# A first load split over two queues, a last batch left in one part and a new table of ranks in a relu² attention kernel with adapters

## The chip, the cores and the metric

The kernel runs on one core of a Trainium2 chip. TensorE (PE in the rows) does the matmuls and writes PSUM. VectorE (DVE) and ScalarE (ACT) read PSUM and do all elementwise work. GpSimd (POOL) and SyncE (SP) issue transfers, POOL those that cast on the way. The metric is the device time of one execution in microseconds, as the median of several runs.

## What is computed

Eight batches of twelve heads, 448 tokens of 64 values, go through an attention with a squared relu in place of a softmax. The result, 3584 tokens of 768 values, goes through eight adapters of rank 16, of which each token takes its two best.

```python
scores = q @ k.transpose(0, 1, 3, 2) / sqrt(64)
attn   = np.maximum(scores, 0.0) ** 2 / 448
x      = (attn @ v).transpose(0, 2, 1, 3).reshape(3584, 768)
logits = x @ w_gate                       # 8 experts
w      = softmax of the two largest logits
out    = x + sum over the two of  w * ((x @ A[e]) @ B[e])
```

## The kernel before

The program is a list of small operations (`build`). Each has the engines that may do it, a duration that the planner assumes, what it depends on, buffers that it takes and gives back, and a rank. `schedule` (L78) walks through time with these assumed durations and hands each free engine the ready operation with the lowest rank. What comes out is a fixed order of instructions for each engine. Each engine then runs its own row strictly in that order. Transfers have their place in the rows of SP, ACT or POOL.

A batch has three "quads" of four heads; a tile of q, k or v is one quad (128 partitions, 2 x 448 values). For each quad:

- **Load** (L250): POOL issues two casting transfers, one for each half of the partitions, float32 in memory to bf16 on chip. The very first q and k are done otherwise (`first`, L263): two float32 transfers each, q from SP and k from ACT, and then a cast, q on VectorE, k on ScalarE (L274).
- **Transposes** (L353): 28 small matmuls for q, 28 for k, into one pair of PSUM banks, copied out by VectorE in one piece (L362). The first quad is copied out in two pieces, q by VectorE and k by ScalarE (L368).
- **QK** (L394): seven steps `j`, each four matmuls of 64 x 448 into a pair of banks. **Relu** (L414 on ScalarE, L416 on VectorE) takes such a pair, 128 x 896, to bf16. **Square** (L432, VectorE) does two steps at once, 128 x 1792.
- **PV** (L449): seven steps accumulate in another pair of banks, which is copied to `xt`, one bank at a time (L473).

For each token tile of 128 (28 tiles, `gate` and `outputs`): the gate matmuls (L490), a chain of small operations on VectorE with a sigmoid on ScalarE between them (L511 to L534), a transpose of the weighted low-rank values (L555) copied out as `zT` (L568), then the output stage: 24 small matmuls that put `x` into a pair of banks (L587), the float32 matmuls with B on top (L602), two copies to `osb` (L621), and the stores from SP (L632). One tile at a time may hold the banks of the output stage (`cap`, "o": 1).

The eight banks are shared by all of this; QK may hold up to three pairs. In the last batch the 448 query columns are cut into 320 and 128 (`PARTS`): all three quads run first for the 320 and then for the 128, so that token tiles 24 to 26 can be finished while the 128 are still being worked on.

Of the kernel before, what the change touches and what calls it, by code (L numbers as in the profile page):

```python
# [9 lines left out]
F32 = mybir.dt.float32  # L10
BF16 = mybir.dt.bfloat16
# [15 lines left out]
PARTS[NB - 1] = ((0, 320), (320, S))  # L27

C = dict(
    slack=0.24419, switch=0, third=5.2529, dve_relu=0.32574, relu_until=400, qk=-3.132, sq=6, pv=5.6586,  # L30
    xt=6.5598, tp=-15.842, tpe=5.1552, gate_mm=0, gate=-6.1261, zt=11.533, zte=14, id=0.77356, out=3.6939,
    pace=6.4673,
)
POOLS = dict(qT=5, a1=4, a2=9, zp=2, zT=3, osb=6, w=3, q=4, k=4, v=6)

MODE_SWITCH = 0.27
HOP = 0.05
LAT = {"PE": 0.165, "ACT": 0.19, "DVE": 0.084, "POOL": 0.0, "SP": 0.0}
# [28 lines left out]
class Dma:  # L67


    def __init__(self, rate=0.33, fixed=2.0):  # L70
        self.rate, self.fixed, self.free = rate, fixed, 0.0

    def land(self, t, mb):
        self.free = max(self.free, t + 0.9) + mb / self.rate
        return self.free + self.fixed - 0.9


def schedule(ops, c=C):  # L78
# [5 lines left out]
    level = dict(POOLS)  # L84
    freed = {b: 0.0 for b in range(8)}
    used = {"s": 0, "t": 0, "p": 0, "m": 0, "y": 0, "o": 0}
    cap = {"s": 3, "t": 1, "p": 2, "m": 2, "y": 1, "o": 1}
# [17 lines left out]
    def choose(o):  # L105
# [3 lines left out]
        slots = sorted((x for x in range(0, 8, 2) if x in freed and x + 1 in freed),  # L109
# [11 lines left out]
        busy = 4 - len(slots) - used["s"]  # L121
        if not slots or busy >= 2:
            return None
# [25 lines left out]
    while left:  # L149
# [9 lines left out]
        for e in free:  # L159
# [6 lines left out]
            if e == "PE":  # L166
                if mode is not None and o.mode != mode:
                    st += MODE_SWITCH
                mode = o.mode
# [25 lines left out]
            for u in o.users:  # L195
                u.missing -= 1
                u.ready = max(u.ready, st if u.after is o else back)
# [19 lines left out]
def build(k=None, c=C):  # L217
# [32 lines left out]
    def load(b, w, q, deps):  # L250
# [8 lines left out]
        o = op(("POOL",), 1.3, fn, deps=deps, kind="load", take=(nm,))  # L259
# [3 lines left out]
    def first(w):  # L263

        nm = "qkv"[w]
        eng = ("SP", "ACT")[w]

        def dma():
            for g in range(2):
                (nc.sync, nc.scalar)[w].dma_start(out=k.raw[w][g * PH : g * PH + PH],  # L270
                                                  in_=k.qkv[w][0, g, :, 0:2, :])

        def cast(cp):
            cp(new(nm, (nm, 0, 0), [128, 2, S], BF16), k.raw[w])  # L274

        d = op((eng,), 0.8, dma, kind="load", rank=-50.0)
        d.mb = 4 * S * 64 * 4e-6
        if w == 0:
# [516 lines left out]
```

## Time and profile before

| | us |
|---|---|
| median of 3 runs (202.75 to 203.67) | 203.2 |
| time of the profiled execution | 201.0 |
| its span, first to last instruction | 199.2 |
| first relu starts | 13.92 |
| last QK matmul ends | 181.53 |
| last relu ends | 181.96 |
| last output copy ends | 194.50 |

Shares of busy time over the whole span: TensorE 81%, VectorE 84%, ScalarE 83%. The granted TensorE clock is 0.999 of full speed on average. Idle time of an engine in these rows has a releaser: the instruction or transfer that ended the wait.

### The profile page before, as it was taken

The page shows a single profiled execution, that of the slowest core. Times are in us where ns is not written, and L with a number is a line of the kernel's source. Part 1 is how long each engine was busy: PE and PEld are TensorE (multiplying, and loading weights), DVE is VectorE, ACT ScalarE, POOL GpSimd, SP SyncE. Part 2 cuts the span into 40 slices and gives each one's busy share as a digit, 9 for nine tenths or more (in the row PEclk, how much of TensorE's full clock was granted, in tenths as well). Part 3 has the DMA queues.
Part 4 walks back from the last instruction along what each step waited for, and adds up shares of the span by engine and source line. Part 5 has one row for each costly group of instructions (what it writes and reads, how often), then busy time and mean ns, then how long its engine had stood idle before and what let it go on. Part 6 is the DMA issues. An engine that isn't in the chain of part 4 may idle for free.

```text
span 199.2 us, 10411 instructions
## 1 busy us (share of the span) xinstructions
PE 162.1 (81%) x4664; PEld 109.0 (55%) x4664; DVE 166.6 (84%) x278; ACT 164.5 (83%) x254; POOL 87.9 (44%) x150
## 2 busy tenths in 40 slices
PE   0056887685999799979987999799999999999990
PEld 0043665363667366646654666466655576585650
DVE  0039999898999999799989999999899799896830
ACT  0167957999999899989999999989999999795330
POOL 8339978989856265726364445642200000000000
PEclk9999999999999999999999999999999999999999
DMA  5997999999999988998899959996540450543655
GB/s 129 225 207 88 141 170 181 160 194 172 178 160 219 206 113 133 225 201 110 144 191 198 126 110 198 213 146 134 129 89 3 121 125 3 143 103 81 164 132 189
DMA packets 26733, 29.66 MB, mean 149 GB/s; under 512 B 4416, under 2 KB 22848, under 8 KB 26688
## 3 DMA queue, kind: packets, MB, share of 16 engines
q0 software_dynamic: 21344, 16.27, 59.1%
q1 hardware_dynamic: 5056, 12.26, 22.0%
q8 instruction: 36, 0.59, 1.3%
q10 hardware_dynamic: 288, 0.46, 0.9%
q14 instruction: 9, 0.07, 0.1%
HBM read 34.23 MB, written 11.01 MB: 227 GB/s over the span
## 4 chain that ended last, share of the span: by engine, by line
PE 46%; ACT 18%; DVE 18%; issue 8%; DMA 6%; SPq 1%; DVEq 0%; ACTq 0%
ACT a L414 15%; PE ps L602 14%; PE ps L449 12%; PE ps L394 9%; DVE a L432 8%; DMA raw<-in_q_dram 4%; PE ps L353 3%; PE ps L555 3%; PE ps L587 3%; DVE a L416 2%; DMA out_dram<-osb 2%; ACT osb L621 2%; DVE qT L362 2%; PE ps L490 1%; DVE zT L568 1%
## 5 line engine op out<-in xcount | busy, mean ns | idle before, releaser
L414 ACT ACTIVATE a<-ps 128x896 bf16<-128x896 f32 (+2 forms) x178 | 139.7, 879 | 9.8 <-PE ps L394 7.3
L432 DVE TENSOR_TENSOR a<-a 128x1792 bf16<-128x1792 bf16 (+3 forms) x96 | 90.5, 967 | 3.5 <-ACT a L414 3.1
L394 PE MATMUL ps<-qT 64*64 64x448 bf16 (+2 forms) x756 | 68.5, 350 | 13.7 <-ACT a L414 9.4
L394 PEld LDWEIGHTS <-qT 64*64 64x64 bf16 x756 | 30.6, 108 | 36.0 <-issue 25.9
L449 PE MATMUL ps<-a,v 64*64 64x448 bf16 (+2 forms) x756 | 43.8, 329 | 2.7 <-issue 0.9
L602 PE MATMUL ps<-B,zT 64*64 64x384 f32 x448 | 45.8, 489 | 0.0
L256 POOL DMA_DIRECT2D v<-in_v_dram x48 | 28.9, 611 | 34.8 <-PE ps L394 15.3
L256 POOL DMA_DIRECT2D q<-in_q_dram x46 | 27.9, 618 | 13.6 <-PE ps L394 6.3
L449 PEld LDWEIGHTS <-v 64*64 64x64 bf16 x756 | 25.0, 106 | 12.2 <-issue 6.9
L256 POOL DMA_DIRECT2D k<-in_k_dram x46 | 28.1, 627 | 7.2 <-DMA q<-in_q_dram 4.9
L362 DVE COPY qT<-ps 128x1792 bf16<-128x1792 bf16 x23 | 24.9, 1085 | 2.0 <-PE ps L353 1.4
L621 ACT COPY osb<-ps 128x384 f32<-128x384 f32 x38 | 18.7, 549 | 6.8 <-PE ps L602 5.9
L353 PE MATMUL ps<-identb,q 64*64 64x64 bf16 x672 | 12.3, 199 | 12.5 <-DVE q L274 10.4
L473 DVE CAST xt<-ps 128x448 bf16<-128x448 f32 (+2 forms) x38 | 20.7, 568 | 0.8 <-PE ps L449 0.7
L353 PEld LDWEIGHTS <-q 64*64 64x64 bf16 x672 | 11.6, 114 | 17.7 <-DVE q L274 10.4
L602 PEld LDWEIGHTS ps<-B,zT 64*64 64x64 f32 x448 | 16.5, 134 | 4.4 <-issue 3.0
L621 DVE COPY osb<-ps 128x384 f32<-128x384 f32 x18 | 10.0, 555 | 5.8 <-PE ps L602 4.6
L587 PEld LDWEIGHTS <-xt 64*64 64x64 bf16 x672 | 11.0, 108 | 5.3 <-issue 3.5
L416 DVE TENSOR_SCALAR a<-ps 128x896 bf16<-128x896 f32 (+1 forms) x11 | 11.3, 1028 | 2.9 <-PE ps L394 2.9
L490 PE MATMUL ps<-awg,xt 128*128 128x136 bf16 x168 | 13.0, 224 | 0.4 <-DVE osb L621 0.4
L587 PE MATMUL ps<-identb,xt 64*64 64x64 bf16 x672 | 11.7, 194 | 1.0 <-ACT osb L621 0.9
L490 PEld LDWEIGHTS <-xt 128*128 128x128 bf16 x168 | 10.0, 98 | 4.4 <-issue 4.1
(35 smaller groups left out, 96.8 us busy)
## 6 DMA issues: line engine op xcount, KB each, us to landing
out_dram<-osb SPq DMA_DIRECT2D x56, 192.0 KB, 3.7
v<-in_v_dram POOLq DMA_DIRECT2D x48, 112.0 KB, 4.6
q<-in_q_dram POOLq DMA_DIRECT2D x46, 112.0 KB, 4.9
k<-in_k_dram POOLq DMA_DIRECT2D x46, 112.0 KB, 5.2
B<-in_moe_B_dram SPq DMA_DIRECT2D x2, 384.0 KB, 10.1
raw<-in_k_dram ACTq DMA_DIRECT2D x2, 224.0 KB, 5.5
raw<-in_q_dram SPq DMA_DIRECT2D x2, 224.0 KB, 6.3
a_raw<-in_moe_A_dram POOLq DMA_DIRECT2D x1, 192.0 KB, 3.8
```

Source lines behind the costliest of these rows:

```text
L256: nc.gpsimd.dma_start(out=t[g * PH : g * PH + PH], in_=k.qkv[w][b, g, :, 2 * q : 2 * q + 2, :])
L353: nc.tensor.transpose(k.ps_b[sl * PH : sl * PH + PH, m.banks[g], (w * J + j) * PH : (w * J + j) * PH + PH], T["qk"[w], b, q][r, sl, j * PH ...
L362: nc.vector.tensor_copy(t.rearrange("p g w x -> p g (w x)"), k.ps_b[:, m.banks[0] : m.banks[0] + 2, : 2 * S])
L394: nc.tensor.matmul(out=bank(o, sl)[g * PH : g * PH + PH, at : at + w], lhsT=t[r, g, 1, j * PH : j * PH + PH], rhs=t[r, g, 0, x0:x1], start ...
L414: nc.scalar.activation(out, flat(qk_ops[n], w), ACTF.Relu, scale=k.relu_scale)
L432: nc.vector.tensor_mul(a2, T["a1", g0], T["a1", g0])
L449: nc.tensor.matmul(out=bank(head, g)[sl * PH : sl * PH + PH, :w], lhsT=vn[r, sl, j * PH : j * PH + PH], rhs=T["a2", g0][r, i, sl * w : sl ...
L473: evac(w, lambda cp, g=g: cp(k.xt[:, g * QUADS + q, b * S + x0 : b * S + x1], bank(src, g)[:, :w]), deps=[pv_ops[n]], free=[(src, g)], ran ...
L490: nc.tensor.matmul(out=bank(zops[0])[:, t * ZW : t * ZW + ZW], lhsT=k.xt[:, do, 128 * tiles[t] : 128 * tiles[t] + 128], rhs=k.awg[:, do, : ...
L587: nc.tensor.matmul(out=bank(o_id, r)[tok * PH : tok * PH + PH, do * PH : do * PH + PH], lhsT=k.xt[rr, do, c0 + tok * PH : c0 + tok * PH + PH],
L602: nc.tensor.matmul(out=bank(o_id, r)[tok * PH : tok * PH + PH, : DO * PH].rearrange("p (o d) -> p o d", o=DO), lhsT=T["zT", g0][rr, zi, h, ...
L621: cp(T["osb", tl].rearrange("p (o r d) -> p r o d", r=2, d=PH)[:, r], bank(o_id, r)[:, : DO * PH].rearrange("p (o d) -> p o d", o=DO))
```

## The change

- **First q and k.** q alone comes uncast, its two halves from two queues (SP and ACT, one transfer each), and VectorE casts it. The first k becomes an ordinary casting load on POOL, ahead of the others. The transposes of the first k are cut into 3 and 4 steps, and VectorE copies them out in two pieces, after q's.
- **Sigmoid's table.** A sigmoid of eight values stands at the head of ScalarE's row (`warm`), so that the table it needs is loaded there; the later load goes.
- **Last batch.** `PARTS` no longer cuts it.
- **xt copies.** Up to step 147 the two banks of a PV result are copied by one instruction.
- **Output stage.** Two tiles may hold banks there (`ocap=2`).
- **B.** In the planner its load depends on that of A.
- **Buffers and ranks.** `a1` 4 to 5, `a2` 9 to 12, all ranks new, assumed durations and the assumed speed of transfers changed, a successor on the same engine may follow at once.

```diff
-PARTS[NB - 1] = ((0, 320), (320, S))
 C = dict(
-    slack=0.24419, switch=0, third=5.2529, dve_relu=0.32574, relu_until=400, qk=-3.132, sq=6, pv=5.6586,
...
+    a12=(5, 12), merge_x=147, merge_o=0, ocap=2, sqs=(2,), slack=0.032648, switch=3.8275, third=6,
+    dve_relu=0.39442, relu_until=400, qk=-5.753, sq=6.7076, pv=4.9427, xt=7.7968, tp=-16.052,
...
-POOLS = dict(qT=5, a1=4, a2=9, zp=2, zT=3, osb=6, w=3, q=4, k=4, v=6)
+POOLS = dict(qT=5, a1=C["a12"][0], a2=C["a12"][1], zp=2, zT=3, osb=6, w=3, q=4, k=4, v=6)
...
-    cap = {"s": 3, "t": 1, "p": 2, "m": 2, "y": 1, "o": 1}
+    cap = {"s": 3, "t": 1, "p": 2, "m": 2, "y": 1, "o": c.get("ocap", 1)}
...
+    def first():
+        def dma(eng, g):
+            eng.dma_start(out=k.raw[g * PH : g * PH + PH], in_=k.qkv[0][0, g, :, 0:2, :])
+        def warm():
+            nc.vector.memset(k.warm, 0.0)
+            nc.scalar.activation(k.warm, k.warm, ACTF.Sigmoid)
+        ds = [op(("SP",), 0.8, lambda: dma(nc.sync, 0), kind="load", rank=-50.0),
+              op(("ACT",), 0.8, lambda: dma(nc.scalar, 1), kind="load", rank=-50.0)]
+        op(ACT, 1.4, warm, rank=-49.0)
...
+        if (b, q) == (0, 0):
+            cut, evs = 3, []
+            m1 = op(PE, 0.1, lambda: mm(1, 0, cut), deps=[loaded[b, 1, q], m], after=m, mode="64", kind="tp",
...
+            for i, (d, x0, x1) in enumerate(((m, 0, S), (m1, S, S + cut * PH), (m2, S + cut * PH, 2 * S))):
+                evs.append(op(DVE, dve(2 * (x1 - x0), 1.92), lambda x0=x0, x1=x1: piece(x0, x1),
...
+        if n < c["merge_x"]:
+            return [
+                evac(2 * w, lambda cp: cp(k.xt[:, q::QUADS, b * S + x0 : b * S + x1], pair(src)[:, :, :w]),
+                     deps=[pv_ops[n]], free=[(src, 0), (src, 1)], rank=pv_ops[n].rank + c["xt"])
+            ]
...
-    b_load = op(("SP",), 0.8, b_fn, kind="load")
...
+            b_load = op(("SP",), 1.4, b_fn, deps=[a_load], kind="load")
```

The start of ScalarE's row before (a name's number is its buffer; `waits` names the engine or transfer queue whose semaphore it waits for):

```order
L270 DMA raw_104<-in_k_dram 64x2x448 x2
L274 ACT_TABLE_LOAD [waits DMAHW2_49]
L274 CAST k_0_162<-raw_104 128x896 [waits DMAHW0_49]
L368 COPY qT_0_160<-ps 128x2x448 [waits DVE_49,PE_49]
L414 ACTIVATE a_0_211<-ps 128x896 [waits PE_49]
```

The same place now:

```order
L273 DMA raw<-in_q_dram 64x2x448
L277 ACT_TABLE_LOAD
L277 ACTIVATE warm<-warm 1x8 [waits DVE_49]
L429 ACTIVATE a_0_205<-ps 128x896 [waits PE_49]
L429 ACTIVATE a_2_239<-ps 128x896 [waits PE_49] x2
```

k's cast and its copy have left ScalarE, and the table load stands ahead of all data and waits for none. On SP one transfer of q is left; B's two follow it directly in both rows, without a wait.

POOL's loads at the start, before:

```order
L256 DMA q_1_118<-in_q_dram 64x2x448 x2
L256 DMA k_1_121<-in_k_dram 64x2x448 x2
L256 DMA v_0_124<-in_v_dram 64x2x448 x2
L256 DMA q_2_157<-in_q_dram 64x2x448 x2
L256 DMA k_2_164<-in_k_dram 64x2x448 [waits DMASW0_49]
L256 DMA k_2_164<-in_k_dram 64x2x448 [waits DMASW1_49]
```

And now:

```order
L262 DMA k_0_116<-in_k_dram 64x2x448 x2
L262 DMA q_1_119<-in_q_dram 64x2x448 x2
L262 DMA k_1_122<-in_k_dram 64x2x448 x2
L262 DMA v_0_155<-in_v_dram 64x2x448 x2
L262 DMA q_2_189<-in_q_dram 64x2x448 [waits DMASW0_49]
L262 DMA q_2_189<-in_q_dram 64x2x448 [waits DMASW1_49]
```

The first k stands in the place that q of the second quad had; every later load has moved back by one place. The ninth transfer waits for the first to land, in both.

The end of ScalarE's row before, from its last relus (`sg` is the sigmoid of a gate, `zT` and `osb` the copies around the output stage):

```order
L414 ACTIVATE a_188_5110<-ps 128x256
L621 COPY osb_5120<-ps 128x6x64
L527 ACTIVATE sg_5180<-t_5174 128x16
L527 ACTIVATE sg_5186<-t_5182 128x8
L621 COPY osb_5198<-ps 128x6x64
L473 CAST xt<-ps 128x128 x2
L527 ACTIVATE sg_5323<-t_5321 128x8
L621 COPY osb_5341<-ps 128x6x64
L568 COPY zT_5344<-ps 128x2x2x64
L621 COPY osb_5388<-ps 128x6x64
L621 COPY osb_5427<-ps 128x6x64
L621 COPY osb_5464<-ps 128x6x64
```

And now:

```order
L429 ACTIVATE a_166_4807<-ps 128x896 x2
L648 COPY osb_4846<-ps 128x6x64
L648 COPY osb_4885<-ps 128x6x64
L493 CAST xt<-ps 128x448
L648 COPY osb_4924<-ps 128x6x64
L547 ACTIVATE sg_4988<-t_4978 128x16
L547 ACTIVATE sg_4996<-t_4992 128x8
L648 COPY osb_5016<-ps 128x6x64
L648 COPY osb_5101<-ps 128x6x64
L648 COPY osb_5168<-ps 128x6x64
L648 COPY osb_5205<-ps 128x6x64
L648 COPY osb_5214<-ps 128x6x64
```

Six output copies stood behind the last relu, now eight do, and the gates of the last four tiles come behind the last full-width `xt` copy.

## Rows read from the trace of the kernel before

**Rows 1.** Stretches: length, busy us (count) of each engine, granted clock, transfer share, GB/s

```profile
13.90:182.00 168.10, 148.44 (x4259) 100.00 (x4255) 157.59 (x247) 156.88 (x238) 80.56 (x133) 1.00 0.85 144
24.00:35.00 11.00, 8.94 (x288) 6.62 (x285) 11.00 (x14) 7.47 (x10) 9.05 (x17) 1.00 1.19 174
```

**Rows 2.** Timeline of the start: start, length, engine, instruction [idle before, releaser]

```profile
9.17 1.28 ACT L274 ACT_TABLE_LOAD   x1 [9.17 <-DMA raw<-in_k_dram]
9.69 0.63 DVE L274 CAST q<-raw 128x896 bf16<-128x896 f32 x1 [8.12 <-DMA raw<-in_q_dram]
...
11.02 0.62 DVE L368 COPY qT<-ps 128x896 bf16<-128x896 bf16 x1 [0.70 <-PE ps L353]
...
11.69 0.59 PE L353 MATMUL ps<-identb,k 64*64 64x64 bf16 x28 [0.73 <-DVE qT L368]
12.33 0.91 ACT L368 COPY qT<-ps 128x896 bf16<-128x896 bf16 x1 [0.92 <-PE ps L353]
...
13.28 1.33 PE L394 MATMUL ps<-qT 64*64 64x448 bf16 x12 [1.00 <-ACT qT L368]
```

**Rows 3.** Transfers issued at 0.74: size, us from issue to landing

```profile
raw<-in_k_dram ACTq DMA_DIRECT2D x1, 224.0 KB, 3.5
raw<-in_q_dram SPq DMA_DIRECT2D x1, 224.0 KB, 4.5
```

**Rows 4.** The same view: issued from 1.4 to 2.8, POOL's first three and SP's second, third

```profile
q<-in_q_dram POOLq DMA_DIRECT2D x1, 112.0 KB, 6.4
...
raw<-in_q_dram SPq DMA_DIRECT2D x1, 224.0 KB, 8.0
...
B<-in_moe_B_dram SPq DMA_DIRECT2D x1, 384.0 KB, 9.4
q<-in_q_dram POOLq DMA_DIRECT2D x1, 112.0 KB, 8.1
k<-in_k_dram POOLq DMA_DIRECT2D x1, 112.0 KB, 9.8
```

**Rows 5.** Groups by shape: count, busy us, mean ns of one, idle before and releasers

```profile
L414 ACT ACTIVATE a<-ps 128x896 bf16<-128x896 f32 x137 | 118.8, 977 | 7.9 <-PE ps L394 6.4 <-issue 1.3
L432 DVE TENSOR_TENSOR a<-a 128x1792 bf16<-128x1792 bf16 x73 | 77.4, 1083 | 2.1 <-ACT a L414 1.9
...
L414 ACT ACTIVATE a<-ps 128x640 bf16<-128x640 f32 x21 | 14.0, 710 | 0.9 <-ACT a L414 0.4 <-PE ps L394 0.3
...
L432 DVE TENSOR_TENSOR a<-a 128x1280 bf16<-128x1280 bf16 x10 | 7.8, 818 | 0.4 <-ACT a L414 0.4
...
L414 ACT ACTIVATE a<-ps 128x256 bf16<-128x256 f32 x20 | 7.0, 388 | 1.0 <-PE ps L394 0.7 <-ACT a L414 0.2
...
L432 DVE TENSOR_TENSOR a<-a 128x512 bf16<-128x512 bf16 x10 | 4.1, 423 | 1.0 <-ACT a L414 0.9
```

**Rows 6.** Timeline of ScalarE around the second table load

```profile
34.22 13.20 ACT L414 ACTIVATE a<-ps 128x896 bf16<-128x896 f32 x16 [1.27 <-issue]
47.44 1.28 ACT L527 ACT_TABLE_LOAD   x1
48.73 0.22 ACT L527 ACTIVATE sg<-t 128x24 f32<-128x24 f32 x1
```

**Rows 7.** Who waited for whom: us in total, times, longest

```profile
PE ps L394 <- ACT a L414: 9.4, 23, 0.9
```

**Rows 8.** Timeline of the end

```profile
181.28 0.25 PE L394 MATMUL ps<-qT 64*64 64x128 bf16 x4
...
185.09 0.95 PE L449 MATMUL ps<-a,v 64*64 64x128 bf16 x56
...
186.91 0.38 PE L587 MATMUL ps<-identb,xt 64*64 64x64 bf16 x24
...
187.34 1.52 PE L602 MATMUL ps<-B,zT 64*64 64x384 f32 x16
...
193.94 0.56 DVE L621 COPY osb<-ps 128x384 f32<-128x384 f32 x1 [1.00 <-PE ps L602]
```

More of the change, by code (lines that the diff above doesn't have):

```diff
@@ L108, in choose @@
             return None
-        slots = sorted((x for x in range(0, 8, 2) if x in freed and x + 1 in freed),
+        slots = sorted((x for x in range(0, c.get("nb", 8), 2) if x in freed and x + 1 in freed),
                        key=lambda x: max(freed[x], freed[x + 1]))
@@ L196, in schedule @@
                 u.missing -= 1
-                u.ready = max(u.ready, st if u.after is o else back)
+                u.ready = max(u.ready, st if u.after is o or u.engs == (e,) and o.kind != "load" else back)
                 if not u.missing:
@@ L257, in fn @@
                                     in_=k.qkv[w][b, g, :, 2 * q : 2 * q + 2, :])
-        o = op(("POOL",), 1.3, fn, deps=deps, kind="load", take=(nm,))
+        o = op(("POOL",), 1.17, fn, deps=deps, kind="load", take=(nm, "lane"), give=("lane",))
         o.mb = 4 * S * 64 * 4e-6
         return o
[L263 to L278, printed above, removed]
-            return evac(2 * S, cast, engs=DVE, rate=1.92, deps=[d], take=(nm,), rank=-50.0)
-        return evac(2 * S, cast, engs=ACT, deps=[d], take=(nm,), rank=-50.0)
+    def first():
[7 more added lines that the diff above has]
+        op(ACT, 1.4, warm, rank=-49.0)
+        for d in ds:
+            d.mb = 2 * S * 64 * 4e-6
+        return evac(2 * S, lambda cp: cp(new("q", ("q", 0, 0), [128, 2, S], BF16), k.raw), engs=DVE, rate=1.92,
+                    deps=ds, take=("q",), rank=-50.0)
     def sel_fn():
@@ L346, in tp, with mm @@
         rank = first_use[b, q] + c["tp"]
-        def mm(w):
-            for j in range(J):
+        def mm(w, j0=0, j1=J):
+            for j in range(j0, j1):
                 for g in range(2):
@@ L615, in outputs, with ev_all @@
         evs = []
-        for r in range(2):
+        def ev_all(cp):
+            cp(new("osb", ("osb", tl), [128, 128 * DO], F32).rearrange("p (o r d) -> p r o d", r=2, d=PH),
+               pair(o_id)[:, :, : DO * PH].rearrange("p r (o d) -> p r o d", d=PH))
+        if tl < c["merge_o"]:
+            evs.append(evac(2 * DO * PH, ev_all, deps=[prev], free=[(o_id, 0), (o_id, 1)], rank=v + c["out"]))
+        for r in range(2) if not evs else ():
             def ev(cp, r=r):
@@ L683, in build @@
     zuse = {g[0]: len(g) for g in groups}
-    xdeps, seen = {}, set()
+    xdeps, seen, nx = {}, set(), {}
     def finish(n):
@@ L693, in finish @@
             xt_ops.setdefault(col, []).extend(x)
+        nx.update({o: 1 / len(x) for o in x})
         for tl in range(NT):
             both = [xt_ops.get(128 * tl + h * 64, []) for h in range(2)]
-            if tl not in xdeps and all(len(x) == 2 * QUADS for x in both):
+            if tl not in xdeps and all(sum(nx[o] for o in x) == QUADS for x in both):
                 xdeps[tl] = list(dict.fromkeys(both[0] + both[1]))
@@ L751 @@
     h.g_raw = const.tile([128, DO, E], BF16)
-    h.raw = [const.tile([128, 2, S], F32, name=f"raw{w}") for w in range(2)]
+    h.raw = const.tile([128, 2, S], F32)
+    h.warm = const.tile([1, 8], F32)
     ctx.enter_context(tc.manual_schedule())
```

69 lines of the change are left out of this document (37 added, 32 removed).

## The prediction

> **What bounds the kernel now.** I read the stretches first. From the first relu (13.9) to the last (182.0) VectorE is busy for 157.6 and ScalarE for 156.9 of 168.1 us, TensorE for 148.4 [rows 1]. So over 84% of the span the two elementwise engines set the pace together, each with about 11 us of idle time. Much of ScalarE's idle time lies in one place: from 24 to 35 it works 7.5 of 11 us while VectorE works all 11 [rows 1]. The waits agree: QK waits 23 times for ScalarE to give back a bank pair, 9.4 us in total [rows 7]. Ahead of that stretch stand 13.9 us in which no relu can run, and behind it 17 us that end the program; there one chain decides. So I take three terms: start, middle, end.
>
> The start, read from the timeline: q's cast waits until 9.69 for q's second half, then come transposes, VectorE's copy to 11.64, k's transposes (they wait for that copy), ScalarE's copy to 13.24, and QK at 13.28 [rows 2]. The table load at 9.17 stands beside this chain: k's cast behind it is done before VectorE's copy lets the k transposes go. The end: after the last QK matmul (181.53) TensorE works nearly without a gap, a tile every 1.75 us, to 193.93; then copies to 194.50 and stores to 199.2 [rows 8].
>
> **Start: -2.6 us.** Both first halves that were issued at 0.74, one from each queue, landed 3.5 and 4.5 us later [rows 3]; q's second half, behind the first on SP, took 8.0 from 1.56 [rows 4]. Now q's halves are the first ones of their two queues. So q lands at 0.74 + 4.5 = 5.25 instead of 9.6. Cast 0.63, transposes 0.59, copy 0.62 [rows 2] and three handovers of 0.05, as between 11.64 and 11.69, end at 7.25. Then k decides, since it comes through POOL. POOL's first load took 6.4 us for one half and 8.1 for the other [rows 4], issued at 1.43 and about 2.1: landed at 7.8 and 10.2. That is the late bound for k, which takes this place. For the early bound, q's own path (7.25) lets the k transposes start at once. B is not moved: the planner's new dependence gives no wait in SP's row, B follows q directly and is in flight with k (before, its first half landed 9.4 us after its issue [rows 4]). But k's float32 halves, 448 KB that shared the engines with POOL's first load, are gone from the other queues. I take 9.0, nearer to the late bound because B stays. From there: transposes 0.59, the two pieces copied by VectorE 0.62 in all, three handovers, 1.4 together: QK at 10.4 instead of 13.28, a gain of 2.9. The bounds are 10.2 + 1.4 = 11.6, a gain of 1.7, and 7.25 + 1.4 = 8.65, a gain of 4.6. The split of the k copies earns nothing: VectorE's second piece has no wait of its own in the order and the first QK waits once, so both come after all 28 transposes; its price is one of the handovers above.
>
> What is queued behind: TensorE's row has the second quad's q transposes after three QK steps. That q stands where the second quad's k stood, which landed at about 2.73 + 9.8 = 12.5 for its first half [rows 4]; without k's float32 bytes ahead of it, earlier. Should it land at 12.5 to 13.5, TensorE stands still for 1 to 2 us, with three relus of 0.98 to cover. That takes back 0 to 1.2; I take 0.3, since the relus ahead of it hide most. So the start gives 2.6, and its low end is 1.7 - 1.2 = 0.5.
>
> **Middle: -3.7 us.** Three things leave it. (a) The cut last batch. A relu of 640 and one of 256 hold ScalarE for 14.0/21 + 7.0/20 = 1.02 us, one of 896 for 118.8/137 = 0.87 [rows 5]: 0.15 for each of 21 steps, 3.2 us. Squares: 7.8/10 + 4.1/10 = 1.19 against 77.4/73 = 1.06 [rows 5], ten times 0.13: 1.3 us. (b) The sigmoid's table load, 1.28 us in the middle of a full ScalarE [rows 6]; in its new place, behind the issue of one transfer, some eight idle microseconds of ScalarE hide it until the first relu at about 11. (c) The xt copies: 54 become 27; one instruction less is worth at most the same 0.15, 4.0 us. Together 9.8 us of work on two engines that share it, 4.9 each. That is the upper end, because it takes every instruction as if it stood alone. In a full row they overlap: 16 relus take 13.20 us, (13.20 - 0.98)/15 = 0.815 apart [rows 6], of which 896 x (0.977 - 0.388)/640 per element = 0.82 is already the whole; so the fixed cost of one instruction in a full row may be near nothing. The order also moves three relus and four output copies from ScalarE's row to VectorE's, which gives up as much in xt copies; that shifts work between two engines that are equally full, and I cost it at nothing. Lower end: (b) and half of (a), 3.5 us, 1.8 each. I take 3.7, in the upper half, because the groups of the last batch do have waits between their short pieces, 0.9 to 1.0 us each for three of the four [rows 5], and because fewer relus are given to VectorE early, where it alone is full [rows 1].
>
> More `a1` and `a2` buffers and new ranks change who waits, not the work, and I cost them at nothing. They could win back at most the 3.5 us that ScalarE idles between 24 and 35, half of it in time; what they could lose is the third rival.
>
> One rule is to be weighed here. The rows show 1.28 us for the load, the relus ending at 47.42 ahead of it and the sigmoid starting at 48.73, right behind [rows 6]. The Trainium skill, "ScalarE: Activation LUTs", section "What ACT_TABLE_LOAD costs", puts a drain of about 1.38 us on top, 2.66 in all. By the page another 0.7 us would go from the middle, and the sum would be 198.9. This trace has no room for the drain, and I stay with the row.
>
> **End: +2.7 us.** All of token tiles 24 to 27 now wait for the last PV. Counting TensorE's row after its last QK: 7 instead of 5 blocks of 24 small matmuls (0.38 each), 7.5 instead of 6 tiles of B matmuls (1.52 each), 4 instead of 3 gates (six matmuls of 136 columns, taken as a block of small ones, 0.38), and 28 PV matmuls of 448 instead of 56 of 128 (0.95) [rows 8]; by columns that is 12,544 against 7,168, 0 to 0.7 more, I take 0.4. Sum: 0.76 + 2.28 + 0.38 + 0.4 = 3.8. Against it, the last QK now is followed by up to two full relus (0.98 each) instead of short ones, while TensorE has output work to do: counted from the last relu about 1.1 less. So 2.7, from 1.5 (if more of it hides under the last squares) to 4.5 (if the gate's chain of small operations, which now has one tile of output work to hide under, shows). The last copy and the store stay: 0.56 and 4.7.
>
> **Sum.** -2.6 - 3.7 + 2.7 = -3.6 us on a span of 199.2: 195.6. The profiled execution took 201.0, 1.8 more than its span, and the median of the runs is 2.2 above that. I take the difference over to the median: 203.2 - 3.6 = **199.6**. Ends of the terms: -0.5 to -4.6, -1.8 to -4.9, +4.5 to +1.5. As they are unlikely to fall together, the forecast's own range is 196.5 to 202.
>
> **The rivals.**
> - *Start gives nothing.* k lands at 10.2 or later beside B, and the second q at 13: start -0.5, sum -1.5, **201.7**. For it: the POOL halves in the rows took 6.4 to 9.8 us [rows 4]. Against: 448 KB fewer in their way. The Trainium skill, "DMA: Bandwidth & Descriptors", section "Issuing engines are not separate DMA queues", says that transfers of all issuers interleave on the same 16 engines; by that the k from POOL shares with B and both q halves, which speaks for this rival. Chance 0.14.
> - *The uncut batch costs its whole tail.* Tiles 24 to 27 are done one after the other behind the gate chain of the last PV, and nothing hides it: neither the 1.1 us of the last relus count, nor the one tile of output work (0.38 + 1.52) that stands ahead of it in TensorE's row. End 3.8 + 1.9 = +5.7, sum -0.6, **202.6**. For it: the chain crosses between VectorE and ScalarE twice. Against: in the order that tile's work does stand there. Chance 0.12.
> - *Slower: bank pairs.* Two tiles in the output stage take two of the four pairs, so QK finds fewer, and ScalarE and VectorE wait. Price: one wait of QK for a pair is 9.4/23 = 0.41 us [rows 7]. From nine such waits more (3.6/0.41) the gain is gone; with one for 16 of the 28 tiles, +6.6: sum +3.0, **206.2**. For it: QK waits for pairs already now. Against: in the order most tiles follow one another with a QK step between their halves. Chance 0.12.
>
> **How the numbers follow.** The forecast has 0.62. About 0.5% (1.0 us) is what a measurement can tell from no change, so faster is below 202.2, slower above 204.2. Faster: 0.60 of the forecast, 0.10 and 0.02 of the first two rivals, 0.72 in all; same: 0.02 + 0.04 + 0.07 + 0.01 = 0.14; slower: 0.03 + 0.11 = 0.14. The range 195.6 to 203.6 leaves out the ends where the early start and the upper end of the middle meet (0.07) and the slower rival with the worst of the second (0.12).
>
> **What would show it.** Start: q's cast at 5.3, first k transposes at 9.0, first QK at 10.4; a first k transpose after 10.2 refutes the term. TensorE's wait for the second q should be under 1 us. Middle: first relu to last relu about 164.4 us, no table load in it; if QK's waits for ScalarE exceed 13 us, the third rival is at work. End: from the last relu to the end of the span about 20 us; 23 or more means the second rival. The forecast is wrong if the middle stretch is not shorter although it holds less work: then the new order, not the work, decides.

## The result

The changed kernel takes 198.5 us (median of 4 runs, 196.5 to 200.2), the one before 203.0 in the same comparison (4 runs, 202.4 to 203.7): a ratio of 0.971, interval 0.966 to 0.977. Here and below, medians are of all runs, while a ratio with its interval compares only the faster runs of both kernels. The forecast was 199.6 and a faster kernel. The profiled execution of the changed kernel took 199.7 us, its span 197.7; a second profile of it, in the experiments, 196.7 and 194.8.

**The start.** Timeline of the changed kernel, the lines that answer to [rows 2]:

```profile
5.45 0.73 DVE L284 CAST q<-raw 128x896 bf16<-128x896 f32 x1 [3.88 <-DMA raw<-in_q_dram]
...
7.54 0.26 PE L362 MATMUL ps<-identb,k 64*64 64x64 bf16 x2 [0.73 <-DVE qT L377]
...
9.80 0.58 PE L362 MATMUL ps<-identb,k 64*64 64x64 bf16 x26 [2.00 <-DMA k<-in_k_dram]
...
10.83 1.33 PE L409 MATMUL ps<-qT 64*64 64x448 bf16 x12 [0.45 <-DVE qT L377]
...
11.47 0.92 ACT L429 ACTIVATE a<-ps 128x896 bf16<-128x896 f32 x1 [8.48 <-PE ps L409]
```

q's cast stands at 5.45 instead of 9.69, two k transposes run at 7.54, and the rest waits 2.0 us for k's second half. The first QK is at 10.83, 13.28 before.

**The stretches.** Length, busy us (count) of PE, PEld, DVE, ACT, POOL, granted clock, transfer share, GB/s. The changed kernel, first relu to last, then 25 to 35 (the early stretch of [rows 1] without its first microsecond), then from the QK of step 42 to that of step 147, from there to the last relu, and the tail:

```profile
11.47:177.10 165.63, 144.82 (x4072) 97.72 (x4068) 154.31 (x216) 152.29 (x207) 81.53 (x136) 0.99 0.86 146
25.00:35.00 10.00, 7.95 (x269) 5.54 (x260) 10.00 (x11) 9.86 (x12) 8.74 (x16) 1.00 1.19 173
...
45.00:155.32 110.32, 95.74 (x2730) 63.53 (x2724) 100.36 (x146) 98.24 (x136) 51.62 (x87) 0.98 0.87 151
155.32:177.08 21.76, 21.17 (x542) 15.12 (x545) 21.26 (x31) 21.76 (x33) 0.00 (x0) 1.00 0.38 93
177.08:197.70 20.62, 14.49 (x369) 9.90 (x360) 8.84 (x29) 5.75 (x15) 0.00 (x0) 0.97 0.59 156
```

The kernel before, the same three stretches by steps:

```profile
51.42:153.10 101.68, 92.89 (x2632) 62.05 (x2631) 97.64 (x149) 98.70 (x143) 46.82 (x79) 1.00 0.88 155
...
153.10:181.95 28.85, 27.09 (x844) 19.21 (x840) 24.81 (x53) 25.45 (x56) 0.00 (x0) 1.00 0.35 85
181.95:199.22 17.27, 11.91 (x350) 7.58 (x342) 7.54 (x30) 4.50 (x14) 0.00 (x0) 0.99 0.61 163
```

ScalarE, which idled a third of the early stretch, now works 9.86 of 10 us there. The last batch takes 21.8 us instead of 28.9, the tail 20.6 instead of 17.3. And the 105 steps in between take 110.3 us instead of 101.7 (107.3 in the second profile), with hardly more work: 198.6 us busy on the two elementwise engines against 196.3. So the gain is a sum of parts of both signs, and one of them, a loss of 8.6, stood in no term.

**The waits.** The changed kernel's row that answers to [rows 7], and TensorE's waits with no releaser:

```profile
PE ps L409 <- ACT a L429: 4.3, 12, 0.6
PE ps L622 <- issue: 3.4, 2, 1.9
PE ps L362 <- issue: 2.5, 2, 1.9
...
PE ps L464 <- issue: 0.9, 1, 0.9
...
PE ps L409 <- issue: 0.6, 1, 0.6
...
PE ps L607 <- issue: 0.6, 1, 0.6
```

QK waits for ScalarE less than half as long as before. But TensorE stands still for 8.0 us, seven times, with nothing that the profile shows it to wait for. In the kernel before there are three such waits, 1.6 us in all:

```profile
PE ps L449 <- issue: 0.9, 1, 0.9
...
PE ps L555 <- issue: 0.5, 1, 0.5
...
PE ps L394 <- issue: 0.2, 1, 0.2
```

### The profile page after: what moved, and what is told of

The parts are those of the page before. It is cut to its first block, busy times and chain, and to the rows that moved or that the text cites. A ratio compares the mean times of both kernels' runs of the same rounds, so it can differ in the third digit from the quotient of the medians.

```text
span 197.7 us, 10002 instructions
## 1 busy us (share of the span) xinstructions
PE 161.4 (82%) x4496; PEld 109.0 (55%) x4496; DVE 165.4 (84%) x251; ACT 159.5 (81%) x222; POOL 88.3 (45%) x152
## 3 DMA queue, kind: packets, MB, share of 16 engines
q1 hardware_dynamic: 4912, 12.03, 21.9%
## 4 chain that ended last, share of the span: by engine, by line
PE 44%; DVE 31%; ACT 9%; issue 7%; DMA 5%; POOL 1%; ACTq 0%; POOLq 0%; SPq 0%; DVEq 0%
DVE a L447 14%; PE ps L622 13%; PE ps L464 11%; PE ps L409 10%; ACT a L429 6%; DVE qT L371 4%; DMA k<-in_k_dram 4%; DVE a L431 3%; PE ps L362 3%; PE ps L575 3%; PE ps L510 3%; PE ps L607 2%; DVE osb L648 2%; DVE xt L489 2%; ACT xt L489 2%
## 5 line engine op out<-in xcount | busy, mean ns | idle before, releaser
L429 ACT ACTIVATE a<-ps 128x896 bf16<-128x896 f32 x154 | 132.7, 948 | 15.8 <-PE ps L409 15.0
L447 DVE TENSOR_TENSOR a<-a 128x1792 bf16<-128x1792 bf16 x84 | 89.1, 1082 | 0.4
L409 PE MATMUL ps<-qT 64*64 64x448 bf16 x672 | 66.7, 376 | 6.8 <-ACT a L429 4.3
L622 PE MATMUL ps<-B,zT 64*64 64x384 f32 x448 | 49.0, 490 | 3.4 <-issue 3.4
L464 PE MATMUL ps<-a,v 64*64 64x448 bf16 x672 | 45.3, 358 | 2.8 <-issue 0.9
L409 PEld LDWEIGHTS <-qT 64*64 64x64 bf16 x672 | 27.3, 109 | 25.5 <-issue 16.7
L262 POOL DMA_DIRECT2D k<-in_k_dram x48 | 29.3, 629 | 5.4 <-DMA q<-in_q_dram 3.5
L648 ACT COPY osb<-ps 128x384 f32<-128x384 f32 x34 | 16.2, 497 | 9.3 <-PE ps L622 7.1
L622 PEld LDWEIGHTS ps<-B,zT 64*64 64x64 f32 x448 | 18.4, 133 | 9.3 <-issue 7.1
L431 DVE TENSOR_SCALAR a<-ps 128x896 bf16<-128x896 f32 x14 | 15.2, 1084 | 1.8 <-ACT osb L648 0.9
L362 PE MATMUL ps<-identb,k 64*64 64x64 bf16 x672 | 11.6, 200 | 4.7 <-DMA k<-in_k_dram 2.0
L362 PEld LDWEIGHTS <-k 64*64 64x64 bf16 x672 | 10.5, 113 | 6.0 <-DMA k<-in_k_dram 3.0
```

The source lines that it names most:

```text
L262: nc.gpsimd.dma_start(out=t[g * PH : g * PH + PH], in_=k.qkv[w][b, g, :, 2 * q : 2 * q + 2, :])
L362: nc.tensor.transpose(k.ps_b[sl * PH : sl * PH + PH, m.banks[g], (w * J + j) * PH : (w * J + j) * PH + PH], T["qk"[w], b, q][r, sl, j * PH ...
L409: nc.tensor.matmul(out=bank(o, sl)[g * PH : g * PH + PH, at : at + w], lhsT=t[r, g, 1, j * PH : j * PH + PH], rhs=t[r, g, 0, x0:x1], start ...
L429: nc.scalar.activation(out, flat(qk_ops[n], w), ACTF.Relu, scale=k.relu_scale)
L431: nc.vector.tensor_scalar(out, flat(qk_ops[n], w), k.relu_scale, 0.0, op0=ALU.mult, op1=ALU.max)
L447: nc.vector.tensor_mul(a2, T["a1", g0], T["a1", g0])
```

## The experiments

The marks used below are read from each trace: the first QK, the QK of steps 42 and 147 (of 168), the last relu, the end. From the first QK to QK 42 is called the ramp, from QK 42 to QK 147 the stretch, from the last relu to the end the tail; "block waits" are TensorE's waits with no releaser, summed over the profile from such rows; why they have this name is shown further down.

| kernel | first QK | to QK 42 | stretch | to last relu | tail | block waits |
|---|---|---|---|---|---|---|
| before | 13.3 | 38.1 | 101.7 | 28.9 | 17.3 | 1.6 |
| before, again | 11.9 | 40.0 | 103.8 | 29.3 | 17.0 | 3.0 |
| before, 64 instructions ahead | 11.9 | 39.0 | 105.9 | 28.4 | 17.0 | 3.9 |
| changed | 10.8 | 34.2 | 110.3 | 21.8 | 20.6 | 8.0 |
| changed, again | 10.2 | 35.0 | 107.3 | 21.8 | 20.6 | 5.8 |
| old start | 11.8 | 34.1 | 110.0 | 21.9 | 19.9 | 7.3 |
| table late | 10.4 | 35.5 | 105.5 | 21.8 | 20.2 | 3.8 |
| B behind | 8.2 | 35.1 | 105.9 | 21.8 | 20.2 | 4.5 |
| changed, 64 ahead | 11.1 | 34.5 | 108.5 | 21.8 | 20.0 | 7.8 |
| V once | 10.9 | 33.8 | 101.6 | 21.8 | 20.4 | 0.7 |
| cut back | 10.6 | 34.6 | 106.8 | 31.3 | 13.3 | 5.3 |
| old ranks | 10.8 | 37.3 | 108.0 | 21.4 | 22.3 | 6.5 |
| spaced | 8.6 | 39.2 | 103.9 | 21.8 | 20.5 | 2.4 |
| spaced late | 8.7 | 37.5 | 104.6 | 21.8 | 20.4 | 3.9 |

A straight line through the 14 pairs of stretch and block waits gives a stretch of 100.6 us without such waits and 1.16 us more for each microsecond of them; the correlation is 0.98. These sums hold waits outside the stretch too: inside it the three profiles of the kernel before have only 0.2, 0.5 and 2.1 us of them, the two of the changed kernel 7.9 and 5.5. With the waits inside alone the line is 101.9 us and 1.01 us more for each, correlation 0.94. That is the theory: **what the stretch lost is TensorE's waiting for its own instructions.** The rival was that the new order itself is slower there.

**The changed kernel again.**

> The changed kernel once more, as the reference of this set. Theory: the gain is made of the start (about 2.5 us), the middle (more than the 3.7 us forecast) against a longer end; expected ratio to the kernel before 0.968 to 0.976, first QK at 10.8, first relu to last relu 163 us (165.6 in the profile of the changed kernel, which has a gap of TensorE of 1.9 us at 53). Rival: the gap at 53 is part of this program's order; then it stands there in every profile, at the same instruction.

198.4 us (6 runs, 196.7 to 203.5; 0.983 of the kernel before, 0.977 to 0.989): less of a gain than the 0.968 to 0.976 that was expected, while the way from the first relu to the last, 163.4, came as expected. First the changed kernel, then this profile of it, TensorE's timeline around the longest wait:

```profile
52.36 0.81 PE L622 MATMUL ps<-B,zT 64*64 64x384 f32 x5
55.09 0.54 PE L622 MATMUL ps<-B,zT 64*64 64x384 f32 x2 [1.91 <-issue]
```

```profile
52.45 0.81 PE L622 MATMUL ps<-B,zT 64*64 64x384 f32 x5
55.67 0.54 PE L622 MATMUL ps<-B,zT 64*64 64x384 f32 x2 [2.40 <-issue]
```

The wait is at the same instruction, longer by half a microsecond. Counting TensorE's weight loads and matmuls, all seven waits of the changed kernel stand at instructions whose number is 190 more than a multiple of 256. In all 14 profiles of this document it is 74 of the 77 such waits; the other three are 0.2 us each. Such a place is called a border, and the 256 instructions between two borders a block. The page's part on queues says what moves in such portions: 0.57 MB in 35 packets, 16 KB each.

```profile
q8 instruction: 35, 0.57, 1.3%
```

Behind this wait TensorE's clock fell. Stretches of this profile ahead of the wait's end and behind it:

```profile
47.00:55.60 8.60, 5.74 (x209) 3.88 (x204) 8.60 (x11) 6.77 (x9) 6.96 (x12) 1.00 1.12 189
55.60:60.00 4.40, 4.15 (x51) 2.55 (x53) 1.37 (x2) 2.53 (x4) 3.56 (x6) 0.64 1.22 201
```

The granted clock behind the 2.4 us is 0.64 in the mean, so 1.2 GHz for most of these 4.4 us; VectorE works 1.4 us there and ScalarE 2.5. So a long block wait can cost more than itself. It does not always: of the two waits of 1.9 us in the first profile the one at 55 was followed by a fall of the clock and the one at 130 was not, and in the second profile of the kernel before, below, the clock is 0.50 from 50.0 to 53.4 with no block wait near it, behind 4 us in which TensorE was busy for 1.9.

**The old start.** q whole from SP and k whole from ScalarE's queue, float32, ScalarE casts k; the rest as changed.

```diff
-            eng.dma_start(out=k.raw[g * PH : g * PH + PH], in_=k.qkv[0][0, g, :, 0:2, :])
+            for g in range(2):
+                eng.dma_start(out=k.raw[w][g * PH : g * PH + PH], in_=k.qkv[w][0, g, :, 0:2, :])
...
+            nc.scalar.copy(new("k", ("k", 0, 0), [128, 2, S], BF16), k.raw[1])
```

> The changed kernel with the first transfers as before: q whole from SP and k whole from ACT in float32, ScalarE casts k, POOL begins with q of the second quad. The rest of every engine's row is kept. Theory: the start is worth what the first relu shows, 2.4 to 2.6 us, since the elementwise engines are full from there on and nothing catches up; ratio to the changed kernel 1.012 to 1.014. Rival: a later start is caught up in the first 35 us, because there ScalarE has idle time; then under 1 us, ratio below 1.005.

198.7 us (196.5 to 199.5; 0.980, 0.972 to 0.988). The first QK is at 11.75: 0.9 and 1.5 later than in the two profiles of the changed kernel, not the 2.4 to 2.6 of the theory, and at QK 42 it is 0.8 and 0.6. The loads are worth no more than that. In the runs' time it can't be seen.

**The table load back in the middle.** The early activation is a relu, so that the sigmoid's table is loaded ahead of the first gate.

```diff
-            nc.scalar.activation(k.warm, k.warm, ACTF.Sigmoid)
+            nc.scalar.activation(k.warm, k.warm, ACTF.Relu)
```

> The changed kernel with a relu in place of the sigmoid in the first small instruction, so that the sigmoid's table is loaded again at the first gate; nothing else moves. Theory by the row of 1.28 us, shared by two engines: 0.6 us, and up to 1.3 if ScalarE is the one that is late there; ratio to the changed kernel 1.003 to 1.0065. Rival (a drain of 1.4 us that the rows do not show): 1.3 to 2.7 us, ratio up to 1.0135.

198.5 us (195.3 to 200.3; 0.977, 0.970 to 0.985). ScalarE's timeline of this run:

```profile
37.58 3.53 ACT L429 ACTIVATE a<-ps 128x896 bf16<-128x896 f32 x4
41.13 1.28 ACT L547 ACT_TABLE_LOAD   x1
42.42 0.22 ACT L547 ACTIVATE sg<-t 128x24 f32<-128x24 f32 x1
```

The relus end at 41.11, the sigmoid starts at 42.42, so the load takes 1.3 in ScalarE's row, and QK 35 to QK 42 take 8.7 us against 7.2 and 7.6 in the two profiles of the changed kernel (of the 8.7 the last microsecond lies at a granted clock of 0.50, so not all of the difference need be the load's). In the runs' time it can't be told. The Trainium skill, "ScalarE: Activation LUTs", section "What ACT_TABLE_LOAD costs", adds a drain of about 1.4 us; here as in [rows 6] there is no room for it, and the measurement decides.

**B behind V.** B's two loads are issued by GpSimd behind the third V load, at 17.1.

```diff
-                nc.sync.dma_start(out=k.B2[r * PH : r * PH + PH],
+                nc.gpsimd.dma_start(out=k.B2[r * PH : r * PH + PH],
```

> The changed kernel with B's two transfers issued by POOL behind v of the third quad, instead of by SP right behind q; the other rows are kept. Theory: B is what held the first k until 9.80, so the second half of the first k lands by 7.5 to 8.5, first QK at 8.7 to 9.6, and the kernel is 1.2 to 2.1 us faster than the changed one. Rival: k is late because of POOL's own path; then it lands at 9.5 to 9.8 as now, and the time is the same within 0.5 us.

198.7 us (193.3 to 200.6; 0.979, 0.970 to 0.987). Timeline of the start:

```profile
7.17 0.59 PE L362 MATMUL ps<-identb,k 64*64 64x64 bf16 x28 [0.72 <-DVE qT L377]
...
8.21 0.19 PEld L409 LDWEIGHTS <-qT 64*64 64x64 bf16 x8 [0.59 <-DVE qT L377]
```

All k transposes run as soon as q's copy lets them; the first QK is at 8.2, 2.0 to 2.6 earlier, and at QK 42 1.7 to 1.9 of it are left, as the theory has it. So k's second half was late because of B. The runs' times hide these 2 us too: they lie 7 us apart.

**The borders moved.** 64 TensorE instructions more at the start, while it has nothing to do.

```diff
+    for i in range(32):
+        nc.tensor.matmul(out=h.ps[0:1, 7, i : i + 1], lhsT=h.identb[0:64, 0:1],
+                         rhs=h.identb[0:64, 0:1], start=True, stop=True)
```

> The changed kernel with 64 more TensorE instructions at its very start (32 weight loads and 32 matmuls of one column, into a bank that nothing uses yet, while TensorE has nothing else to do). Nothing else is moved. In the profile of the changed kernel TensorE stands still several times with no releaser ('issue'), 0.5 to 1.9 us each, about 8 us in all, and each time at an instruction whose number in TensorE's row is 190 more than a multiple of 256; the instruction queue q8 moves 16 KB for 256 instructions. Theory (a block of 256 instructions did not arrive in time): the waits leave the instructions at which they stood (none any more at the B matmul of L622 near 55, nor at the one near 104) and stand 64 instructions earlier in the program, at the q or k transposes of L362 near 52, at the identity matmuls of L607 near 101. Their sum can be larger or smaller, 2 to 9 us, so the time lies anywhere from 194 to 201. Rival (the waits belong to what stands there, such as the first matmul of a group into a bank): they stay at the matmul of L622 near 55 and near 104, with 1 to 3 us.

198.0 us (4 runs, 194.1 to 200.5). TensorE's timeline around 55, and its waits with no releaser:

```profile
52.53 0.23 PE L362 MATMUL ps<-identb,k 64*64 64x64 bf16 x4
55.85 0.38 PE L362 MATMUL ps<-identb,k 64*64 64x64 bf16 x23 [3.09 <-issue]
```

```profile
PE ps L362 <- issue: 5.5, 5, 3.1
PE ps L607 <- issue: 1.3, 1, 1.3
PE ps L409 <- issue: 1.0, 1, 1.0
```

No matmul of B (L622) waits any more; the wait stands 64 instructions earlier, in the middle of k's transposes. The rival of this run, that the wait belongs to the matmul, falls: it belongs to the border. Behind this wait, the longest of the three shown so far, the clock did not fall:

```profile
55.85:60.25 4.40, 4.04 (x128) 3.01 (x128) 3.15 (x4) 3.73 (x6) 2.76 (x5) 1.00 1.13 181
```

**V loaded once.** V is loaded for the first batch alone, and the other seven read it again; the kernel leaves out their own V, so its result is another one.

```diff
+            if w == 2 and b:
+                T[nm, b, q] = T[nm, 0, q]
+                return
```

> The changed kernel with the same row on every engine, only that V is loaded for the first batch alone and read again for the other seven, which takes 42 of the 142 casting loads (some 4.7 MB) away; so the attention of batches 1 to 7 is that of another V. Theory (the instruction block waits its turn among the data transfers): the blocks' waiting time from the crossing of one border to the start of the next fetch falls from a mean of about 2 us between 40 and 140 us to about 1, and the waits of TensorE with no releaser fall from about 8 us (5 in a second profile of the same kernel) to under 2; the stretch from the QK of step 42 to that of step 147, 107 to 110 us, falls to 102 to 105, and the time to 192 to 196. Rival (the waits come from the program's own density, however quiet the transfers are): they stay at 5 to 8 us and the time at 198.

190.2 us (4 runs, 189.2 to 190.5; 0.943, 0.938 to 0.949), more of a gain than the theory's 192 to 196. The one wait with no releaser, and the stretch:

```profile
PE ps L625 <- issue: 0.7, 1, 0.7
```

```profile
44.69:146.26 101.57, 93.23 (x2727) 62.19 (x2724) 99.54 (x146) 97.50 (x136) 30.93 (x52) 1.00 0.67 121
```

With the same row of instructions and three tenths of the casting loads gone, TensorE's waits are gone and the stretch takes 101.6 us, as in the kernel before. So the changed order is not slower by itself, and the waits depend on the transfers. The four runs lie within 1.3 us, where those of most other kernels are 3 to 7 apart; so a part of the spread of the runs, too, may be these waits, which no run shows apart from that of the clock.

The trace keeps the packets of the instruction queue, and they tell how a block comes late. Nearly every packet starts after TensorE has gone over a border, takes about 1 us, and is for the next border. The four longest waits of the changed kernel (us):

```
border   packet starts   packet ends   TensorE reaches the next border   goes on at
 49.4        52.7           53.8                   52.7                     55.1
 98.0       101.3          102.9                  102.3                    104.2
113.2       116.6          117.6                  117.7                    118.9
123.5       127.2          128.2                  127.6                    129.7
```

TensorE goes on 1.3 to 1.5 us after the packet's end; over the 74 waits at a border in all profiles it is 1.2 to 1.6 us, but for one of 0.7. That ties each of these waits to its packet. From 40 to 140 us a packet starts 2.3 us after the border in the mean and 3.8 at most; a block lasts 5.0, and 4.6 without TensorE's wait at its end. Delay, packet and the 1.4 together are 4.7 in the mean, so a block has nothing to spare. In the run with V loaded once the mean delay of a packet is 1.4, in the three profiles of the kernel before 1.6, 1.8 and 1.9. The Trainium skill, "Runtime: NRT & Kernel Launch", section "Instruction fetch mechanics", has the 16 KB blocks of 256 instructions and their fetch during the block ahead, and calls the crossing's cost mostly hidden; the traces agree on the blocks, not on the cost.

**The last batch cut again**, in 320 and 128 columns, with the changed ranks, planned anew.

```diff
+PARTS[NB - 1] = ((0, 320), (320, S))
```

> The changed kernel with the last batch cut again in 320 and 128 columns, as before the change; ranks, buffers and start as changed, and the plan is made anew. Theory of the prediction (the cut costs its work, 3.2 us of relus and 1.3 of squares on two engines, 2.2 in time, and spares 2.7 at the end): the stretch from the QK of step 147 to the last relu, 21.8 in the changed kernel and 28.9 in the one before, is 23 to 24.5, the tail from the last relu to the end 17 to 18 instead of 20.6; time within 1.5 us of the changed kernel. Rival (the stretch of 28.9 was mostly the cut: two rounds over the 21 steps, two rounds of waits for 640 and 256 columns): it is 27 to 29, the tail 17 to 18, and the kernel 2 to 4 us slower than the changed one.

200.4 us (10 runs, 196.5 to 203.7; 0.980, 0.973 to 0.987). From QK 147 to the last relu, and the tail:

```profile
152.03:183.30 31.27, 30.14 (x865) 21.66 (x865) 27.23 (x62) 27.54 (x63) 0.00 (x0) 1.00 0.42 104
183.30:196.60 13.30, 7.91 (x209) 4.16 (x208) 3.88 (x13) 3.14 (x10) 0.00 (x0) 0.92 0.63 152
```

The cut costs 9.5 us ahead of the last relu and saves 7.3 behind it: in this profile both sides of the prediction's trade are real and far larger than forecast, and larger than either side expected here; uncutting wins 2.2. The ratios of the runs, 0.980 and 0.983 for the changed kernel, don't show that.

**The old ranks**: the table of ranks, `a1` and `a2` of 4 and 9, and one output tile, as before; all else as changed.

```diff
-    a12=(5, 12), merge_x=147, merge_o=0, ocap=2, sqs=(2,), slack=0.032648, switch=3.8275, third=6,
...
+    a12=(4, 9), merge_x=147, merge_o=0, ocap=1, sqs=(2,),
+    slack=0.24419, switch=0, third=5.2529, dve_relu=0.32574, relu_until=400, qk=-3.132, sq=6, pv=5.6586,
...
```

> The changed kernel with the table of ranks, the buffers (a1 of 4, a2 of 9) and the one output tile of the kernel before; start, uncut last batch, merged xt copies and the table load as changed. It tells whose the gain of 3.7 us from the first QK to that of step 42 is, and whose the loss of 4 to 9 us between steps 42 and 147. Theory (the new ranks and the larger pools bring both: ScalarE fuller from 25 to 35, and denser pieces of TensorE that outrun its instruction blocks): first QK to step 42 takes 37 to 38 us as before (34.2 in the changed kernel), steps 42 to 147 take 101 to 104 with waits of TensorE without a releaser under 3 us, time 195 to 200. Rival (the gain in the ramp comes from the start and the merged copies, and the loss from nothing in the ranks): 34 to 35 for the first, 107 to 110 for the second.

200.6 us (4 runs, 197.2 to 201.6). Half of each reading holds. The way to QK 42 is 37.3 instead of 33.8 to 35.5, so ranks and buffers, the second output tile among them, bring 2 to 3 us there. But the stretch is 108.0 with 6.5 us of block waits: the old ranks don't bring the old stretch back, and by this profile the loss is not theirs.

**The kernel before, its borders moved, and again.** The same 64 instructions ahead of the kernel before; then that kernel unchanged.

> The kernel before, with the same 64 TensorE instructions more at its start as in the run with the shifted borders; nothing else is moved. In its profile TensorE stands still without a releaser for 1.6 us in all, in the changed kernel's profiles for 4 to 9. Theory (a block of 256 instructions arrives late where the stretch ahead of it is short and its fetch waits long; where the borders fall is luck, and in the kernel before they fall well): with the borders moved, the kernel before has waits without a releaser of 4 to 9 us too, and its stretch from QK 42 to QK 147 goes from 101.7 to 104 to 108; time 204 to 207. Rival (the plan of the kernel before, with its own order of loads and pieces, gives the fetches more room wherever the borders lie): waits under 3 us, 101 to 104 for the stretch, time unchanged.

> The kernel before, unchanged, for a second profile: is what it shows between QK 42 and QK 147 its habit? If so: 101 to 103 us for that stretch, waits of TensorE without a releaser under 2.5 us. If its first profile was a lucky one: 104 to 108 us, with 4 to 8 us of such waits.

With the borders moved: 204.9 us (4 runs, 204.1 to 207.3; 1.021, 1.014 to 1.027). Its waits, and TensorE's timeline at the longest:

```profile
PE ps L394 <- issue: 2.5, 3, 1.5
...
PE ps L353 <- issue: 1.0, 1, 1.0
...
PE ps L490 <- issue: 0.4, 1, 0.4
```

```profile
64.21 0.35 PE L394 MATMUL ps<-qT 64*64 64x448 bf16 x1
66.06 0.38 PE L394 MATMUL ps<-qT 64*64 64x448 bf16 x3 [1.50 <-issue]
```

Instructions that do nothing, in idle time, make the kernel before 2% slower. Its block waits inside the stretch are 2.1 us where they were 0.2 (0.5 in the profile below), so its borders fell well; that this is all of the 2% is not shown. (The added instructions don't move the first QK, 11.9 here and in the profile below. And the waits alone, 3.9 us, are not the whole: the granted clock is 0.91 from 40 to 80 us, where it was 1.00 in the first profile of the kernel before.) Unchanged, it took 202.2 us (2 runs), and its longest wait stands where it stood in the first profile (first that one, then this):

```profile
33.03 0.91 PE L449 MATMUL ps<-a,v 64*64 64x448 bf16 x13 [0.94 <-issue]
```

```profile
33.11 0.91 PE L449 MATMUL ps<-a,v 64*64 64x448 bf16 x13 [1.55 <-issue]
```

In this second profile the stretch is 103.8 and the block waits 3.0, between the two answers that were expected. It also has its first QK at 11.9, as the one with the moved borders has; the 13.3 of the profile that the prediction was made from was a late one.

**Loads spaced**: as with B behind V (behind the third V load here too), and a GpSimd memset of 0.34 us ahead of each half load. Two loads that follow at once are then 1.7 us apart.

```diff
+                if b or q > 1:
+                    nc.gpsimd.memset(k.pause, 0.0)
                 nc.gpsimd.dma_start(out=t[g * PH : g * PH + PH],
```

> The changed kernel with B's two loads behind the first V load on GpSimd (as in the run in which B is behind), and from the third q on a GpSimd memset of 300 elements of one partition ahead of each half of a casting load, about 0.35 us each, so that two loads are 1.9 us apart instead of 1.2 when GpSimd has not to wait. The same transfers, less bunched; the rows of the other engines are the same. Theory (a block's fetch waits longer the more loads were issued just ahead of it): the mean wait from border to fetch between 40 and 140 us falls from 2.0 to 1.5 or less, the waits of TensorE without a releaser from 7.5 to 2 to 5 us, the stretch from QK 42 to QK 147 from 105.9 to 102 to 104, time 193 to 196. Rival 1 (the amount of transfers counts, not their spacing): waits stay at 6 to 9 us, time 197 to 199. Rival 2 (the spaced loads come too late): TensorE waits for landings of q, k or v, 2 us or more in all between 16 and 60 us, and the time is over 199.

196.0 us (6 runs, 195.0 to 197.8; 0.974, 0.969 to 0.979). Block waits 2.4 us, mean delay of a packet 1.7 us instead of 2.0, stretch 103.9. But the loads were late in the ramp, as the second rival said, though the time was not the one that it gave:

```profile
PE ps L364 <- DMA q<-in_q_dram: 2.2, 2, 1.3
...
PE ps L364 <- DMA k<-in_k_dram: 1.9, 2, 1.6
```

**Spaced from batch 3 on** (`if b > 2:` in the same place).

> As the run with spaced loads, but the GpSimd memsets begin only with the loads of batch 3, which are issued from about 42 us on; the earlier loads follow one another as closely as in the changed kernel. In the run with all loads spaced TensorE waited 2.2 us for q's landings and 1.9 for k's, and the stretch from the first QK to that of step 42 took 39.2 us where the run without spacing took 35.1. Expected, if both readings hold (spacing shortens the block waits, and cost the ramp its lead): first QK at 8.2 to 8.6, step 42 at 43 to 44, the stretch from there to step 147 in 102.5 to 105, waits of TensorE without a releaser 2 to 5 us, time 192 to 195. If the gain of the spaced run was chance (its waits without a releaser were 2.4 us by luck of that profile): 197 to 199, stretch 106 to 108, waits 6 to 9.

194.9 us (6 runs, 193.6 to 196.4; 0.969, 0.962 to 0.977), the fastest of all that do the whole work: 7.0 below the kernel before in the same comparison, 3.5 below the changed kernel's medians in the other comparisons. The first QK, the stretch and the time came as expected; QK 42 came at 46.1, 2 to 3 late: TensorE waited 1.4 us there for landings of k and q, and the granted clock was 0.91 from 30 to 40 us and 0.86 from 40 to 46, all with loads that are not spaced yet. In this profile the block waits are 3.9 us, only 0.6 less than with B behind V alone, so it is the median and the narrower spread that speak for the spacing, not this profile. That the two moves together are faster than the changed kernel is shown (all six runs lie below all of its runs). What the spacing adds to B behind V is not: the ratios 0.969 and 0.979 have intervals that overlap, and the fastest run of all, 193.3, is one with B behind V alone.

## Why the prediction was right

**Start: the mechanism right, the size counted from a late profile.** q's cast at 5.45 (forecast 5.3), first QK at 10.8 and 10.2 (10.4), k's second half behind B as the step said. But 2.6 was counted from 13.28. Over three profiles of the kernel before the first QK is at 12.4 in the mean, over seven with the changed start at 10.7: the gain is 1.7. It was left open whether the second quad's q would stop TensorE; no such wait shows.

**Middle: -3.7 forecast, -2.5 and -4.7 in the two profiles, by parts that the prediction did not see.** From the first relu to the last they took 165.6 and 163.4 (forecast 164.4). Behind this stand the ramp with -3.9 and -3.2, the last batch with -7.1, and the stretch between with +8.6 and +5.6, of which the block waits inside it are 7.7 and 5.3. (Against the second profile of the kernel before the same parts are -5.8 and -5.0, -7.5, +6.5 and +3.5: the signs hold, the sizes move by up to 2 us.)
- The step that failed is "who waits, not the work, and I cost them at nothing". In the ramp ranks and buffers were worth 2 to 3 us in the one profile that tries them, more than the bound that the step gave, half of ScalarE's 3.5 idle us.
- The last batch was under-sized. Its two engines were busy for 50.3 of 57.7 us before and for 43.0 of 43.5 now: 7.2 us of work less, and 6.9 us of idle time less, 3.5 in time. The forecast had 4.5 of that work (the rest moved into the tail) and only a share of the waits.
- The table load came as counted. What the merged copies save was not tried by itself. In the stretch, where most of them lie, nothing of it is seen: where block waits are few it takes 101.7 us in the kernel before and 101.6 in the changed one with V loaded once.
- The loss was in no term and no rival: the waits with no releaser. In the page of the kernel before they were three waits of 1.6 us, and "issue" looked like nothing.

**End: +2.7 forecast, +3.3 measured** (20.6 against 17.3, within the bounds 1.5 and 4.5).

**The rivals.** Start gives nothing: no, but its size, -0.5, is 1.2 from the 1.7 that was measured, and the 2.6 is 0.9 from it. The uncut batch costs its whole tail: no, the tail is 20.6, not 23. Bank pairs: refuted, QK's waits for ScalarE fell from 9.4 to 4.3 us. The sign that was to show the forecast wrong, a middle that is not shorter although it holds less work, did show in a part of the middle, the stretch; only the unforeseen gains of the ramp and the last batch covered it.

So the total was right partly by luck: two things that it did not see stood against each other in the middle, about -7 us (ramp and last batch beyond the forecast) and +6 to +9 (the stretch, most of it block waits). What stays open is why blocks are fetched later in the changed kernel, 2.0 and 2.3 us after the border against 1.6 to 1.9, of which the nearest two differ by only 0.1. With the old ranks it is 2.1, with the old start 2.0, so neither of them alone is it. The blocks are also shorter, 4.6 us without the waits against 4.9 to 5.1 in the three profiles of the kernel before, in part because TensorE has 191 instructions more in the stretch; with the old ranks they are 4.9, and the waits are 6.5 all the same. So what a shorter block and a later fetch each cost is open as well; the planner's new order of loads and the merged copies were not tried apart.

## What to carry to other kernels

Read waits with no releaser by where they stand: if they come back at instruction numbers of one remainder in every profile and move when a few idle instructions are put ahead, the engine waits for its instructions. Fewer transfers took them away here; going back to the old table of ranks did not. Split a stage before costing it: a sum that is right can hide parts of both signs. And take a start or a stretch from two profiles where a term hangs on it; between two profiles of one kernel the first QK moved by 1.4 us here.

## What the runs showed of the hardware

- TensorE's instructions come in blocks of 256 (16 KB), one fetch behind each border; in these kernels a fetch began up to 4.8 us after it, and the engine stood still for up to 3.6 us at a border, 0.7 to 8.0 us in all in one execution. It went on 1.2 to 1.6 us after the fetch's packet had ended, but for one wait of 74.
- After such a wait of 2.4 us the granted clock was 0.64 over the next 4.4 us; after one of 3.1 us in another run it was 1.00.
- 64 instructions in idle time made one kernel 2% slower (1.4 to 2.7%); the other was not told apart from what it was (198.0 and 198.4, runs 6 us apart).
- Three tenths of the casting loads less (4.8 MB of 29.4 in all) gave 8.2 us, though no wait for one of them shows in TensorE's row between QK 42 and the end.
